# Pooled attention and MLP on one core: more buffers for the MLP, and attention re-packed and issued in a fixed order between its matmuls

## The chip, the core and the metric

The kernel runs on one core of a Trainium2 chip. The metric is the device time of one execution in microseconds (us). A time quoted alone is the median of that kernel's runs. A ratio is the mean time of one kernel's fast runs over the mean of the other kernel's fast runs of the same rounds on the same chip, with a 95% interval, so it is not quite the ratio of the quoted medians. The kernel before was run again in each batch of experiments; its medians there were 440.1 to 445.5 us, and this is why ratios are given beside times.

Names of engines in the profile: PE is TensorE (PEld its weight loads), DVE is VectorE, ACT is ScalarE, POOL is GpSimd, SP only issues DMA in these kernels. To turn a tile means to transpose it.

## The reference

Keys and values are averaged over groups of 8 tokens, so each head has 576 queries against 72 pooled keys. The attention output goes straight into a two-layer MLP with h - tanh(h) between.

```python
B, H, S, D = 8, 8, 576, 64                     # q, k, v, all float32
k_p = k.reshape(B, H, 72, 8, D).mean(axis=3)   # v_p the same
attn = softmax(scale * q @ k_p.T)              # 576 x 72 for each head
x = (attn @ v_p).transpose(0, 2, 1, 3).reshape(4608, 512)
h = x @ w_in                                   # 512 -> 2048
out = (h - tanh(h)) @ w_out                    # 2048 -> 512, float32
```

The MLP is worked in 9 groups of 512 tokens. A group has a **hidden phase** of 16 blocks (four matmuls of 512 columns, a tanh, a subtraction) and an **output phase** of four tiles (16 matmuls of 512 columns each, a copy, a store). This makes 9 x (64 + 64) = 1152 matmuls. A token group can start when the attention output of its tokens lies transposed in `xT`.

## The kernel before

An automatic scheduler orders each engine's instructions. The pools of buffers that matter have one buffer each:

```python
tpool = ctx.enter_context(tc.tile_pool(name="tpool", bufs=1))    # t_sb, tanh
opool = ctx.enter_context(tc.tile_pool(name="opool", bufs=1))    # o_sb
ps_h = ctx.enter_context(tc.tile_pool(name="ps_h", bufs=2, space=bass.MemoryType.PSUM))
ps_o = ctx.enter_context(tc.tile_pool(name="ps_o", bufs=1, space=bass.MemoryType.PSUM))
```

Attention casts q, k and v to bf16 on VectorE, adds four of the eight tokens of a group there, and finishes the pooling with small matmuls against a pooling matrix. It turns q and x on TensorE, and works head by head:

```python
for hp in range(NHP):                     # pairs of heads
    ... matmul k_s1 x PT2, k_bf x PTt     # pooled k, transposed
    ... matmul PT2 x v_s1, PTt x v_bf     # pooled v
    for c in range(NQCH):
        nc.tensor.transpose(qT_ps[...], q_bf[...], ident_bf16[...])
for h in range(H):                        # scores: 72 x 576 for each head
    nc.tensor.matmul(sT_ps[:, s0:s0+n], lhsT=kpT_tiles[hp][pr, :], rhs=qT_tiles[hp][pr, s0:s0+n], ...)
    nc.scalar.activation(out=E_sb[:, :], in_=sT_ps[:, 0:S], func=ACT.Exp, scale=scale)
for qb in range(5):                       # values, 65 columns for each head
    for h in range(H):
        nc.tensor.matmul(x_ps[:rows, h, 0:D+1], lhsT=E_tiles[h][:, s0:s0+rows], rhs=vp_tiles[hp][:, h2, :], ...)
    ... reciprocal, product, four transposes of x, copy into xT
```

```python
for i in range(NHID):                     # hidden phase of a group
    hT_ps = ps_h.tile(...)
    ... four matmuls
    t_sb = tpool.tile([128, TG], FP32, name="t_sb", tag="t_sb")
    nc.scalar.activation(out=t_sb[:, 0:ntok], in_=hT_ps[:, 0:ntok], func=ACT.Tanh)
    gT = gpool.tile([128, TG], BF16, name="gT", tag=f"g{i}")
    nc.vector.tensor_sub(out=gT[:, 0:ntok], in0=hT_ps[:, 0:ntok], in1=t_sb[:, 0:ntok])
```

The softmax here doesn't subtract the row's maximum and nothing guards it: scores larger than these inputs give would overflow.

## Time and profile before

| | before |
|---|---|
| time, median of the first 3 runs | 437.9 us |
| span of the profiled run | 439.6 us |
| first MLP matmul | 65.8 us |
| a hidden block of the last group | every 1.41 us |
| an output tile of the last group | every 4.33 us |

The prediction below shows the lines that this table rests on. In the list of waits a line gives the engine and tile that waited, what ended the wait, the total in us, the number of times and the longest. The list for the kernel before:

```profile
DVE rden L277 <- PE x_ps L269: 21.1, 22, 4.0
DVE vp_aug L225 <- ACT kpT_sb L219: 11.1, 11, 3.0
```

Both are waits of VectorE for attention work of TensorE and ScalarE, and both are small against the 107.9 us that it waited for the tanh.

### The profile page before, as it was taken

The numbers are of one execution on the slowest core, as the hardware profiler recorded it, in microseconds if no ns is written. First come the engines' busy times: TensorE is split into PE (matmuls) and PEld (weight loads), VectorE is DVE, ScalarE is ACT, GpSimd is POOL, SyncE is SP. The second block draws the span as 40 slices with busy tenths as digits, with TensorE's granted clock in tenths as the row PEclk, the third lists the DMA queues.
The fourth block names the chain that finished last, engine by engine and source line by source line (L and its number), as shares of the span: only waits on it lengthen the run. The fifth ranks groups of instructions, "written<-read, shape, count | busy, mean of one in ns | idle before, by whom it ended". The sixth has DMA issues, their size and how long they took to land.

```text
span 439.6 us, 5253 instructions
## 1 busy us (share of the span) xinstructions
PE 361.8 (82%) x2048; PEld 163.7 (37%) x2048; DVE 200.9 (46%) x336; ACT 183.6 (42%) x349; POOL 30.7 (7%) x76
## 2 busy tenths in 40 slices
PE   0006479899799989989999997999999898898875
PEld 0002253444345434544444443444543343333322
DVE  1312656864647544862396339244513523513510
ACT  1003335564366326524562463266535534423321
POOL 7401101100100200020000000000000000000000
PEclk9999999999999989999999998999999999999999
DMA  8999994911930391094002101100011021011012
GB/s 211 227 234 249 317 318 137 264 41 49 275 96 0 74 278 67 2 249 171 0 1 60 38 0 25 48 26 0 26 48 25 0 49 48 0 49 48 1 32 65
DMA packets 34329, 42.29 MB, mean 96 GB/s; under 512 B 1792, under 2 KB 28416, under 8 KB 34304
## 3 DMA queue, kind: packets, MB, share of 16 engines
q1 hardware_dynamic: 30464, 34.61, 28.1%
q0 software_dynamic: 3840, 7.34, 8.5%
q8 instruction: 16, 0.26, 0.3%
q14 instruction: 9, 0.07, 0.1%
HBM read 36.70 MB, written 9.44 MB: 105 GB/s over the span
## 4 chain that ended last, share of the span: by engine, by line
PE 56%; DMA 14%; ACT 13%; DVE 11%; SPq 3%; issue 2%; ACTq 0%; DVEq 0%
PE o_ps L350 22%; PE hT_ps L325 19%; DMA k_raw<-in_k_dram 8%; DVE gT L339 7%; DMA out_dram<-o_sb 7%; ACT t_sb L333 6%; PE sT_ps L245 4%; ACT o_sb L358 3%; SPq L121 3%; PE qps L211 3%; PE x_ps L269 2%; PE xT_ps L286 2%; ACT E_sb L254 1%; PE qps L195 1%; PE qps L202 1%
## 5 line engine op out<-in xcount | busy, mean ns | idle before, releaser
L350 PE MATMUL o_ps<-w2b,gT 128*128 128x512 bf16 x576 | 153.1, 383 | 16.4 <-ACT o_sb L358 11.6
L339 DVE TENSOR_TENSOR gT<-hT_ps,t_sb 128x512 bf16<-128x512 f32 x144 | 99.1, 688 | 143.9 <-ACT t_sb L333 107.9
L325 PE MATMUL hT_ps<-xT,w1b 128*128 128x512 bf16 x576 | 151.1, 385 | 8.4 <-DVE gT L339 8.0
L333 ACT ACTIVATE t_sb<-hT_ps 128x512 f32<-128x512 f32 x144 | 85.6, 595 | 49.1 <-DVE gT L339 42.1
L350 PEld LDWEIGHTS <-gT 128*128 128x128 bf16 x576 | 56.2, 98 | 86.3 <-issue 20.0
L325 PEld LDWEIGHTS <-w1b 128*128 128x128 bf16 x576 | 51.3, 98 | 62.2 <-issue 19.6
L358 ACT COPY o_sb<-o_ps 128x512 f32<-128x512 f32 x36 | 21.1, 586 | 89.4 <-PE o_ps L350 60.7
L254 ACT ACTIVATE E_sb<-sT_ps 72x576 bf16<-72x576 f32 x64 | 41.3, 646 | 33.4 <-PE sT_ps L245 33.3
L245 PE MATMUL sT_ps<-qT_sb,kpT_sb 64*72 64x512 bf16 (+1 forms) x128 | 32.2, 320 | 7.5 <-ACT E_sb L254 7.0
L292 ACT COPY xT<-xT_ps 128x512 bf16<-128x512 bf16 (+1 forms) x40 | 21.8, 544 | 25.9 <-PE xT_ps L286 25.5
L269 PE MATMUL x_ps<-vp_aug,E_sb 72*128 72x65 bf16 (+1 forms) x320 | 28.7, 203 | 0.6 <-ACT E_sb L254 0.6
L279 DVE TENSOR_TENSOR x_sb<-x_ps,rden 128x512 bf16<-128x512 f32 (+1 forms) x40 | 27.4, 685 | 0.8
L219 ACT CAST kpT_sb<-qps 128x72 bf16<-128x72 f32 x32 | 6.9, 217 | 49.1 <-PE qps L211 48.0
L181 PE MATMUL qps<-PT,k_s 128*128 128x64 bf16 x32 | 6.5, 204 | 25.0 <-DVE k_s L162 21.5
L269 PEld LDWEIGHTS <-E_sb 72*128 72x128 bf16 (+1 forms) x320 | 18.8, 104 | 16.6 <-issue 12.1
L245 PEld LDWEIGHTS <-kpT_sb 64*72 64x72 bf16 x128 | 11.1, 114 | 35.0 <-issue 34.5
L211 PE MATMUL qps<-ident_bf,q_bf 128*128 128x128 bf16 (+1 forms) x160 | 22.7, 238 | 0.0
L233 ACT COPY qT_sb<-qps 128x576 bf16<-128x576 bf16 x32 | 20.4, 636 | 4.4 <-DVE vp_aug L225 4.4
L143 DVE CAST k_bf<-k_raw 128x2048 bf16<-128x2048 f32 x8 | 9.8, 1227 | 23.3 <-PE qps L188 11.7
L277 DVE RECIPROCAL rden<-x_ps 128x8 f32<-128x8 f32 (+1 forms) x40 | 8.1, 202 | 21.2 <-PE x_ps L269 21.1
L286 PE MATMUL xT_ps<-ident_bf,x_sb 128*128 128x128 bf16 (+1 forms) x160 | 15.7, 224 | 0.9 <-DVE x_sb L279 0.9
L188 PE MATMUL qps<-PTt,k_bf 64*128 64x8 bf16 x32 | 5.7, 179 | 12.0 <-DVE k_bf L147 12.0
(37 smaller groups left out, 153.3 us busy)
## 6 DMA issues: line engine op xcount, KB each, us to landing
q_raw<-in_q_dram SPq DMA_DIRECT2D x8, 1024.0 KB, 6.2
k_raw<-in_k_dram SPq DMA_DIRECT2D x8, 1024.0 KB, 13.1
v_raw<-in_v_dram SPq DMA_DIRECT2D x8, 1024.0 KB, 13.8
out_dram<-o_sb SPq DMA_DIRECT2D x40, 128.0 KB, 2.4
out_dram<-o_sb SPq DMA_DIRECT2D x16, 256.0 KB, 2.3
w1b<-in_moe_w_in_dram POOLq DMA_DIRECT2D x4, 512.0 KB, 13.7
w2b<-in_moe_w_out_dram POOLq DMA_DIRECT2D x4, 512.0 KB, 20.6
q_raw<-in_q_dram POOLq DMA_DIRECT2D x8, 128.0 KB, 7.7
```

The costliest lines, as they stand in the source:

```text
L211: nc.tensor.transpose(qT_ps[:, c * 128 : c * 128 + rows], q_bf[:rows, c, h0 : h0 + 2, :].rearrange("p h d -> p (h d)"), ident_bf16[:rows, ...
L245: nc.tensor.matmul(sT_ps[:, s0 : s0 + n], lhsT=kpT_tiles[hp][pr, :], rhs=qT_tiles[hp][pr, s0 : s0 + n], start=True, stop=True,)
L254: nc.scalar.activation(out=E_sb[:, :], in_=sT_ps[:, 0:S], func=ACT.Exp, scale=scale,)
L269: nc.tensor.matmul(x_ps[:rows, h, 0 : D + 1], lhsT=E_tiles[h][:, s0 : s0 + rows], rhs=vp_tiles[hp][:, h2, :], start=True, stop=True,)
L279: nc.vector.tensor_mul(out=x_sb[:rows, :, :], in0=x_ps[:rows, :, 0:D], in1=rden[:rows, :, :].to_broadcast([rows, H, D]),)
L286: nc.tensor.transpose(xT_ps[:, fb, 0:rows], x_sb[:rows, 2 * fb : 2 * fb + 2, :].rearrange("p h d -> p (h d)"), ident_bf16[:rows, :rows],)
L292: nc.scalar.copy(out=xT[:, :, pos0 : pos0 + rows], in_=xT_ps[:, :, 0:rows],)
L325: nc.tensor.matmul(hT_ps[:, 0:ntok], lhsT=w1b[:, fb, i * 128 : (i + 1) * 128], rhs=xT[:, fb, tok0 : tok0 + ntok], start=(fb == 0), stop=(f ...
L333: nc.scalar.activation(out=t_sb[:, 0:ntok], in_=hT_ps[:, 0:ntok], func=ACT.Tanh,)
L339: nc.vector.tensor_sub(out=gT[:, 0:ntok], in0=hT_ps[:, 0:ntok], in1=t_sb[:, 0:ntok],)
L350: nc.tensor.matmul(o_ps[:brows, :], lhsT=gts[i][:, tb * 128 : tb * 128 + brows], rhs=w2b[:, i, :], start=(i == 0), stop=(i == NHID - 1),)
L358: nc.scalar.copy(out=o_sb[:brows, :], in_=o_ps[:brows, :])
```

## The change

The intent is to let TensorE run the MLP without bubbles, to give attention fewer and fuller matmuls, and to spread the next batch's attention through the MLP of the present group in an order that is written down. The core of the diff, with cuts:

```diff
-    tpool ... bufs=1    opool ... bufs=1    ps_h ... bufs=2    ps_o ... bufs=1
+    tpool ... bufs=3    opool ... bufs=3    ps_h ... bufs=3    ps_o ... bufs=2    ps_a ... bufs=3
+    ctx.enter_context(tc.manual_schedule())        # program order on every engine
...
+    k_rows = k.rearrange("b h (g j) d -> b (h g) (j d)", j=POOL)   # a row: 8 tokens of one group
+    def pool_kv(b, ke, ve):                        # pooling by adds; GpSimd for b >= 1
+        for eng, r in ((ke, kr), (ve, vr)):
+            eng.tensor_tensor(out=r[:, :, 0:4, :], in0=r[:, :, 0:4, :], in1=r[:, :, 4:8, :], op=ALU.add)
+            eng.tensor_tensor(out=r[:, :, 0:2, :], in0=r[:, :, 0:2, :], in1=r[:, :, 2:4, :], op=ALU.add)
+            ...                                    # last add into kd; for v a product with a 0/1 mask into VB
+    def q_prep(b):
+        nc.vector.tensor_copy(...)                 # cast, two instructions
+        for j in range(R + 1):
+            nc.sync.dma_start_transpose(out=qT[...], in_=q_bf[...])
+    def scores(b, t):                              # 128 (head, group) rows at once, two halves of 288 queries
+        for n, hp in enumerate(PAIRS[t]):
+            nc.tensor.matmul(ps[:, :], lhsT=KB[b % 2][:, hp, t*128:(t+1)*128], rhs=qT[:, hp, ...], ...)
+    def av(b, blk):                                # values, four heads at once
+        ...                                        # reciprocal, product
+        nc.sync.dma_start_transpose(out=xT[...], in_=x_sb[...])
...
+    load_kv(0); load_q(0)
+    pool_kv(0, nc.vector, nc.gpsimd)
+    ...                                            # GpSimd: w1 in four pieces, w2 in four
+    q_prep(0)
+    load_kv(1); load_q(1)                          # SP: behind the transposes of q
+    k_transpose(0); scores(0, 0..4); av(0, 0..4)   # SP: transposes of x behind load 1
+    for g in range(NG):
+        for i in range(NHID):
+            mlp_h(g, i, gts)
+            if i == 1: pool_kv(nb, nc.gpsimd, nc.gpsimd)
+            if i == 3: q_prep(nb); load_kv(nb + 1); load_q(nb + 1)
+            if i == 13: k_transpose(nb)
+        for u in range(16):                        # quarters of the output tiles
+            mlp_o(...)
+            if u < NT: scores(nb, u)
+            if u in (6, 7, 9, 10, 12): av(nb, ...)
```

## The prediction

The forecast's sum came to 341 us, given as 340: start 42, slow first matmuls 2, MLP 248.3, attention on TensorE 31.5, q casts 10, x transposes 3.5, tail 3.6.

- The 31.5 is 7 x 4.5, and the 4.5 was 1.96 for the scores, 2.1 for the values and 0.4 for k. The 2.1 is cut. The trace of the changed kernel shows 0.36 us for the six value matmuls of a block (117.39 to 117.75 us), so 1.8 us for five blocks. The 122 ns of a score matmul stands: in proportion to 0.2155 us for 512 columns it is 0.121 us, and that trace shows four in 0.49 us (112.72 to 113.21 us), 0.1225 us each.
- Of the rivals the reckoning of (a) came to 440 us, and of the first half of (b), 350 us or more. That adds on GpSimd can block a q cast, the second half of (b), was a guess then, since the trace of the kernel before has no add on GpSimd; `a_vadd_dve` below shows it (a cast of 0.41 us took 1.75 beside the adds).

The 2 to 3 us for a transpose by DMA were the author's estimate, from the 2.4 us that a plain 128 KB store takes to land in the kernel before (issue list); the even shares of the engines were an assumption.

> **What bounds the kernel now.** I read the page first: the engines' shares, the chain that ended last, the costliest groups, the slices.
>
> ```profile
> PE 361.8 (82%) x2048; PEld 163.7 (37%) x2048; DVE 200.9 (46%) x336; ACT 183.6 (42%) x349; POOL 30.7 (7%) x76
> PE   0006479899799989989999997999999898898875
> DMA  8999994911930391094002101100011021011012
> PE 56%; DMA 14%; ACT 13%; DVE 11%; SPq 3%; issue 2%; ACTq 0%; DVEq 0%
> L350 PE MATMUL o_ps<-w2b,gT 128*128 128x512 bf16 x576 | 153.1, 383 | 16.4 <-ACT o_sb L358 11.6
> L339 DVE TENSOR_TENSOR gT<-hT_ps,t_sb 128x512 bf16<-128x512 f32 x144 | 99.1, 688 | 143.9 <-ACT t_sb L333 107.9
> L325 PE MATMUL hT_ps<-xT,w1b 128*128 128x512 bf16 x576 | 151.1, 385 | 8.4 <-DVE gT L339 8.0
> L333 ACT ACTIVATE t_sb<-hT_ps 128x512 f32<-128x512 f32 x144 | 85.6, 595 | 49.1 <-DVE gT L339 42.1
> ```
>
> PE looks 82% busy, but a matmul's 383 ns is its latency, not its spacing: the reader has to look at the timeline to see how far PE is from full. The list of waits says who holds whom: tanh and subtraction hold each other.
>
> ```profile
> DVE gT L339 <- ACT t_sb L333: 107.9, 98, 3.3
> ACT t_sb L333 <- DVE gT L339: 42.1, 59, 1.2
> ```
>
> The timeline of the last group (no attention left) shows the loop, and further down the output matmuls.
>
> ```profile
> 408.77 1.02 PE L325 MATMUL hT_ps<-xT,w1b 128*128 128x512 bf16 x4 [0.18 <-DVE gT L339]
> ...
> 408.81 0.60 ACT L333 ACTIVATE t_sb<-hT_ps 128x512 f32<-128x512 f32 x1 [0.82 <-DVE gT L339]
> ...
> 409.44 0.69 DVE L339 TENSOR_TENSOR gT<-hT_ps,t_sb 128x512 bf16<-128x512 f32 x1 [0.72 <-ACT t_sb L333]
> ...
> 410.18 1.02 PE L325 MATMUL hT_ps<-xT,w1b 128*128 128x512 bf16 x4 [0.17 <-DVE gT L339]
> ...
> 427.16 3.61 PE L350 MATMUL o_ps<-w2b,gT 128*128 128x512 bf16 x16 [0.72 <-ACT o_sb L358]
> ...
> 431.49 3.61 PE L350 MATMUL o_ps<-w2b,gT 128*128 128x512 bf16 x16 [0.72 <-ACT o_sb L358]
> ```
>
> Sixteen back-to-back matmuls take 3.61 us, so one takes (3.61 - 0.383) / 15 = 0.215 us. A hidden block (four matmuls) should take 0.862 us of PE, but blocks come every 410.18 - 408.77 = 1.41 us: t_sb has one buffer, so the next tanh waits for the subtraction (0.60 + 0.69 + about 0.12 of handover). An output tile comes every 431.49 - 427.16 = 4.33 us instead of 3.45, as o_ps has one buffer. 144 x 1.41 + 36 x 4.33 = 359 us; the first MLP matmul starts at 65.8 us (timeline); with 4 us of tail that makes 429 of the 439.6. So three things bound it: the one-buffer loops, the start (DMA at 8-9 tenths for six slices), and attention work that partly fills the bubbles.
>
> [...]
>
> **The change part by part.**
>
> *MLP.* t_sb and hT_ps get three buffers, o_ps two. The round trip of one hidden buffer is 1.03 (matmuls) + 0.03 + 0.60 + 0.03 + 0.69 + 0.05 = 2.43 us; over three buffers 0.81 us, just under PE's 0.862. VectorE needs 0.72 per block, ScalarE 0.63. So PE sets the pace: 1152 x 0.2155 = 248.3 us instead of 359.
>
> *Attention on PE.* The instruction order shows 52 matmuls a batch instead of 112, all with full 128x128 weights; the q and x transposes are gone. Scores: 16 x 122 ns = 1.96 us. Values: per row block twice (130, 195, 65 columns), the small ones at 64 ns (eight 65-column matmuls of before take 0.65 us: (0.65 - 0.20) / 7)[...]. k: six at some 64 ns, 0.4 us. Together 4.5 us a batch. In the fixed order this lies wholly on PE's path: 7 x 4.5 = 31.5 us (batch 0 is in the start).
>
> *Attention elsewhere.* ScalarE: ten exps of 288 columns, about 0.42 us each (between 595 ns at 512 and 646 at 576, 0.8 ns per column), spread over five quarter tiles: hidden. VectorE: reciprocal 0.2 + product of 256 columns 0.42 (half of 685 ns, plus fixed cost), ten pairs a batch: 6.2 us in the output phase where it has nothing else: hidden. The q cast is not hidden: 1.21 + 0.40 us between the fourth and fifth subtraction; slack is 0.862 - 0.69 = 0.17 per block, and 0.16 over the three buffers, so PE stands about 1.4 us: 7 x 1.4 = 10 us. The eight small K copies at block 13 come too late in the phase to stop PE.
>
> *GpSimd.* Per batch 1280 + 640 + 640 (k) and 1280 + 640 + 320 + 960 (v) = 5760 elements[...]. It starts when a load lands, in the middle of a hidden phase, and is over before the next q cast: hidden.
>
> *DMA transposes.* q's are due 11 us later: hidden. x's last block that the next group needs (fourth, at quarter 10) has 5 quarters, 4.7 us, for 1.5 us of VectorE and an estimated 2 to 3 us of DMA: about even. I allow 0.5 us a group, 3.5 us.
>
> *Start.* k, v, q of batch 0 (3.54 MB) come first and alone. Before moved two batches and both weights, 7.1 MB + 8.4 MB as read, in some 49 us: 316 GB/s. So q is there at 2 + 11.5 = 13.5 us, cast and turned at 19, scores to 25, values to 32. But the transposes of x stand in the same queue behind the load of batch 1, which shares the engines with the weights (GpSimd issues those only after adding v, at about 17 us). With even shares its 3.54 MB take 7.1 / 0.316 = 22 us, to about 40; turned x at 42. Weights are then complete by 55, before the output phase (42 + 13.8) is deep. MLP starts at 42 instead of 65.8[...]: before's first blocks show 1.46 us for three matmuls; I add 2 us.
>
> *Sum:* 42 + 2 + 248.3 + 31.5 + 10 + 3.5 + tail 3.6 (copy 0.58, store 2.4, handover) = 341; I say 340.
>
> **The rivals.** (a) *Transposes by DMA too slow.* [...] (b) *GpSimd becomes the bound*: [...] Or its additions block the q cast, some 3 us a group: 360. (c) *VectorE as bound in the hidden phase*: 16 x 0.72 + 1.6 + 1.0 = 14.1 us against 13.8: only what I charged; each further 1 us costs 7. (d) *The start is DMA-bound as before*: if batch 1 and weights must all land, 55 us instead of 42: 353. (e) *All hidden*: casts and transposes cost nothing, the loads go faster: 320.
>
> **Range and chances.** Terms that come from the trace (248 + 4 of tail) are firm; start (36 to 55), stalls (0 to 4 us a group, up to 30) and attention (28 to 36) are not. Upwards there are more ways than down: 320 to 366. Same or slower needs rival (a) nearly in full, or two others at once: 3% each.
>
> **What would show it.** Right: a first MLP matmul near 42 us; hidden blocks every 0.86 us; one gap of 1 to 2 us after the fourth block of groups with attention, released by the subtraction; no waits of PE for output copies; PE's groups above 90% to the end, chain over 80% PE. Wrong: PE's first waits in a group released by a DMA of xT (a), by kd or VB from POOL (b), q casts far over 1.2 us (b), or the first hidden matmul or the first output tile waiting for weights past 50 us (d).

## The result and the profile after

The changed kernel took **351.77 us** (median of 4 runs, 350.74 to 353.21), against 440.12 us for the kernel before in the same rounds. The ratio is 0.7998, with a 95% interval from 0.7938 to 0.8058. The profiled run was fast, with a span of 350.2 us and a mean granted TensorE clock of 0.961 (the share of full clock that the chip granted).

First the page of the changed kernel: busy time of each engine, the 40 slices (8.75 us each; a digit is tenths of busy time, for PEclk tenths of full clock), and the chain that ended last.

```profile
PE 287.7 (82%) x1538; PEld 143.3 (41%) x1568; DVE 166.7 (48%) x361; ACT 139.9 (40%) x293; POOL 106.9 (31%) x72
PE   0007002899989998999999899989998999999994
PEclk9999655899999999999999999999999999999999
PE 75%; DMA 9%; SPq 7%; DVE 5%; issue 2%; ACT 1%; ACTq 0%; DVEq 0%
```

PE stands at 8 or 9 from the eighth slice to the last but one. The share of 82% is the same as before, and this shows how little that share says: before, PE's busy time held the latency of matmuls that stood apart (0.38 us each, while back to back they come every 0.2155 us). What is left lies at the left edge. Seven slices go by before PE is busy, the fourth is a short spell of attention, and the chain has 9% of DMA and 7% of SP's queue. The clock digits fall to 5 while PE waits (0.52 from 36 to 59 us).

Next the costliest groups (line, engine, operation, tiles; then busy us, mean ns of one, idle us before them and who ended most of it), and the waits that answer to those of before.

```profile
L256 PE MATMUL hT_ps<-xT,w1b 128*128 128x512 bf16 x563 | 129.8, 384 | 9.5 <-DVE gT L266 6.2
L276 PE MATMUL o_ps<-w2b,gT 128*128 128x512 bf16 x559 | 134.6, 379 | 0.9
L264 ACT ACTIVATE t_sb<-hT_ps 128x512 f32<-128x512 f32 x144 | 85.2, 597 | 72.1 <-PE hT_ps L256 71.9
```

```profile
DVE x_sb L218 <- DMA xT<-x_sb: 22.9, 7, 20.0
PE s_ps L184 <- DMA qT<-q_bf: 16.4, 2, 9.3
```

The tanh now waits for TensorE (71.9 us) and no longer for the subtraction. Output matmuls were idle for 0.9 us in all, instead of 16.4, of which 11.6 were waits for copies. (The counts 563 and 559 should be 576: some matmul records are missing from this trace.) The new waits are for DMA transposes: one of 20 us for x, and two that together make 16.4 us for q. Yet a transpose is quick when little else is under way, as the issue list says (out<-in, engine, count, median us from issue to landing; the line of qT has the same count and median):

```profile
xT<-x_sb SPq DMA_TRANSPOSE x40, 2.4
```

The timeline of a group in the middle (start, duration, engine, line, operation, count, and in brackets the idle time before it):

```profile
131.83 1.22 DVE L102 CAST q_bf<-q_raw 128x2048 bf16<-128x2048 f32 x1
...
134.03 6.20 PE L256 MATMUL hT_ps<-xT,w1b 128*128 128x512 bf16 x27 [0.88 <-DVE gT L266]
```

The group's only stall is the 0.88 us that the q cast costs. The first hidden matmuls of the nine groups come at 58.98, 94.27, 126.94, 159.62, 192.29, 224.96, 257.63, 290.30 and 317.93 us: a period of 32.67 us with attention, 27.63 without.

The timeline of the start, where the time went:

```profile
13.43 1.64 DVE L102 CAST q_bf<-q_raw 128x2048 bf16<-128x2048 f32 x1 [3.24 <-DMA q_raw<-in_q_dram]
...
15.10 6.51 SPq L109 DMA_TRANSPOSE qT<-q_bf  x5
...
19.27 3.20 POOL L322 DMA_DIRECT2D w1b<-in_moe_w_in_dram  x4
...
25.59 10.63 SPq L91 DMA_DIRECT2D q_raw<-in_q_dram  x1
...
27.74 3.76 PE L184 MATMUL s_ps<-qT,KB 128*128 128x288 bf16 x15 [7.18 <-DMA qT<-q_bf]
...
58.98 0.58 PE L256 MATMUL hT_ps<-xT,w1b 128*128 128x512 bf16 x1 [2.48 <-DMA xT<-x_sb]
```

Read it from the top. q is there at 13.43 us, and most of it is cast at 15.1. SP then needs 6.51 us to issue five transposes. The weights are issued at 19.27, and the fourth and fifth transposes land only when the other fifteen score matmuls can go, at 27.7. SP's last issue of the load of batch 1 takes 10.63 us. Behind it in SP's order stand the transposes of x, whose first is issued at 36.31 us, and the first MLP matmul starts at 58.98.

### The profile page after: what moved, and what is told of

It reads as the page before. It is cut to its first block, busy times and chain, and to the rows that moved or that the text cites. A ratio compares the mean times of both kernels' runs of the same rounds, so it can differ in the third digit from the quotient of the medians.

```text
span 350.2 us, 4472 instructions
## 1 busy us (share of the span) xinstructions
PE 287.7 (82%) x1538; PEld 143.3 (41%) x1568; DVE 166.7 (48%) x361; ACT 139.9 (40%) x293; POOL 106.9 (31%) x72
## 4 chain that ended last, share of the span: by engine, by line
PE 75%; DMA 9%; SPq 7%; DVE 5%; issue 2%; ACT 1%; ACTq 0%; DVEq 0%
PE o_ps L276 35%; PE hT_ps L256 31%; DMA xT<-x_sb 6%; PE s_ps L184 4%; PE x_ps L208 4%; SPq L91 3%; DMA q_raw<-in_q_dram 3%; DVE q_bf L102 3%; SPq L109 2%; DVE gT L266 2%; ACT t_sb L264 1%; SPq L79 1%; SPq L83 1%; DVE q_bf L105 1%; PE kT_ps L155 1%
## 5 line engine op out<-in xcount | busy, mean ns | idle before, releaser
L256 PE MATMUL hT_ps<-xT,w1b 128*128 128x512 bf16 x563 | 129.8, 384 | 9.5 <-DVE gT L266 6.2
L276 PE MATMUL o_ps<-w2b,gT 128*128 128x512 bf16 x559 | 134.6, 379 | 0.9
L264 ACT ACTIVATE t_sb<-hT_ps 128x512 f32<-128x512 f32 x144 | 85.2, 597 | 72.1 <-PE hT_ps L256 71.9
L120 POOL TENSOR_TENSOR k_raw<-k_raw 128x1280 f32<-128x1280 f32 x7 | 20.2, 2888 | 138.9 <-DMA k_raw<-in_k_dram 138.9
L285 ACT COPY o_sb<-o_ps 128x512 f32<-128x512 f32 x36 | 21.1, 586 | 92.7 <-PE o_ps L276 80.9
L218 DVE TENSOR_TENSOR x_sb<-x_ps,rden 128x256 bf16<-128x256 f32 x80 | 34.0, 425 | 25.4 <-DMA xT<-x_sb 22.9
L208 PE MATMUL x_ps<-VB,E 128*128 128x130 bf16 (+2 forms) x240 | 22.2, 228 | 21.0 <-DVE x_sb L218 20.7
L184 PE MATMUL s_ps<-qT,KB 128*128 128x288 bf16 x128 | 23.6, 305 | 16.4 <-DMA qT<-q_bf 16.4
L191 ACT ACTIVATE E<-s_ps 128x288 bf16<-128x288 f32 x80 | 28.9, 412 | 17.0 <-PE s_ps L184 16.6
L208 PEld LDWEIGHTS <-E 128*128 128x128 bf16 x240 | 17.5, 101 | 31.2 <-DVE x_sb L218 22.4
L120 POOL TENSOR_TENSOR v_raw<-v_raw 128x1280 f32<-128x1280 f32 x8 | 23.1, 2886 | 8.4 <-DMA v_raw<-in_v_dram 8.3
L137 POOL TENSOR_TENSOR VB<-v_raw,mask 128x960 bf16<-128x960 f32 x8 | 14.4, 1794 | 0.6
## 6 DMA issues: line engine op xcount, KB each, us to landing
w1b<-in_moe_w_in_dram POOLq DMA_DIRECT2D x4, 512.0 KB, 11.6
```

The source lines that it names most:

```text
L120: eng.tensor_tensor(out=r[:, :, 0:4, :], in0=r[:, :, 0:4, :], in1=r[:, :, 4:8, :], op=ALU.add)
L184: nc.tensor.matmul(ps[:, :], lhsT=KB[b % 2][:, hp, t * 128 : (t + 1) * 128], rhs=qT[:, hp, half * hs : (half + 1) * hs], start=(n == 0), s ...
L191: nc.scalar.activation(out=E[:, t, half * hs : (half + 1) * hs], in_=ps[:, :], func=ACT.Exp, scale=SCALE)
L208: nc.tensor.matmul(ps[:, h0 : h0 + s1 - s0, :].rearrange("p h d -> p (h d)"), lhsT=E[:, t, c0 : c0 + 128], rhs=vb[:, t, s0:s1, :].rearrang ...
L218: nc.vector.tensor_tensor(out=x_sb[:, half, :, :], in0=ps[:, :, 0:D], in1=rden[:, :, :].to_broadcast([128, 4, D]), op=ALU.mult,)
L256: nc.tensor.matmul(h_ps[:, :], lhsT=w1b[:, fb, i * 128 : (i + 1) * 128], rhs=xT[:, fb, tok0 : tok0 + TG], start=(fb == 0), stop=(fb == NFB ...
```

## The experiments

Twelve kernels ran; all gave correct results. Each was built from the changed kernel except `b_tsb3`, which was built from the kernel before. The theory at the outset was: *the loops with one buffer held the kernel before (M); in the changed kernel the start is 17 us too late because the transposes stand in one queue with the load of batch 1 (Q)*. The rivals were that the weights must land in any case (W), that buffers of x hold the start, and that attention's new form brought the gain.

| run | what | time, us | ratio to before | first hidden matmul, us |
|---|---|---|---|---|
| changed kernel | | 351.77 | 0.7998 | 58.98 |
| a_bufs_one | one buffer each again | 437.22 | 0.9806 | 58.83 |
| b_tsb3 | before, three t_sb | 456.71 | 1.0237 | 66.30 |
| a_load1_late | load of batch 1 later | 350.88 | 0.7980 | 47.06 |
| a_xsb5 | five x_sb | 350.22 | 0.7969 | 57.64 |
| a_xpe_start | x of batch 0 on TensorE | 339.81 | 0.7730 | 42.22 |
| a_qcast_pool | q casts on GpSimd | 344.58 | 0.7836 | 59.45 |
| a_pe_turns | all turns on TensorE | 344.28 | 0.7729 | 31.30 |
| a_vadd_dve | v of batch 0 on VectorE | 350.95 (one run) | - | 58.93 |
| a_best | several together | 320.32 | 0.7184 | 28.45 |
| a_best2 | and q of batch 1 on TensorE | 324.24 | 0.7339 | 29.42 |
| a_best3 | and load 2 later | 325.15 | 0.7416 | 28.75 |
| a_best4 | or load 2 by GpSimd | 332.41 | 0.7526 | 28.75 |

### Where the gain comes from: one buffer each again

```diff
-    tpool bufs=3, opool bufs=3, ps_h bufs=3, ps_o bufs=2
+    tpool bufs=1, opool bufs=1, ps_h bufs=2, ps_o bufs=1
```

> The changed kernel with the MLP's buffers as before: t_sb 1, o_sb 1, hT_ps 2, o_ps 1. Theory M (the buffers carry most of the gain): the hidden loop falls back to 1.41 us a block, 144 x 0.55 = 79 us more, output tiles lose up to 0.6 us each, about 20, and the q cast hides in the slack, 6 less: 440 to 450 us. Rival O (the fixed order of the attention carries it): below 400 us.

It took 437.22 us (436.54 to 437.44), ratio 0.9806 (0.9753 to 0.9859). Of the 0.200 that the changed kernel gains on before, 0.181 is gone again. Waits and timeline of this run:

```profile
ACT t_sb L264 <- DVE gT L266: 107.5, 126, 1.5
```

```profile
106.29 1.02 PE L256 MATMUL hT_ps<-xT,w1b 128*128 128x512 bf16 x4 [0.39 <-DVE gT L266]
107.70 1.02 PE L256 MATMUL hT_ps<-xT,w1b 128*128 128x512 bf16 x4 [0.39 <-DVE gT L266]
```

The block comes every 1.41 us, exactly as in the kernel before, and the tanh waits for the subtraction again. In this order of instructions the buffers carry nearly all of the gain; which of the four buffer counts does most was not separated. All the rest of the change, without them, is worth 2%, and that is a balance of a gain and a loss. The last group, without attention, takes 38.3 us here (392.81 to 431.06) and 34.4 in the kernel before (400.68 to 435.10), because the scheduler of the kernel before puts matmuls of the first output tile into the gaps of the hidden loop, and the fixed order doesn't. From the last group of the kernel before:

```profile
409.63 0.38 PE L350 MATMUL o_ps<-w2b,gT 128*128 128x512 bf16 x1
```

### The reverse: three tanh buffers in the kernel before

```diff
-    tpool = ctx.enter_context(tc.tile_pool(name="tpool", bufs=1))
+    tpool = ctx.enter_context(tc.tile_pool(name="tpool", bufs=3))
```

> The kernel before with three t_sb buffers instead of one and nothing else[...]. Theory M: tanh no longer waits for the subtraction, the hidden loop is then held by two hT_ps buffers, 2.43 / 2 = 1.21 us instead of 1.41 a block: up to 29 us off where no attention fills the gap, 412 to 425 us. Rival O: within 2% of 440.

This was a miss: 456.71 us (455.6 to 457.11), 2.4% *slower* than before (ratio 1.0237, 1.0169 to 1.0306). The loop itself did what was expected. Near the end of the timeline of this run four blocks take 4.86 us (from 393.90 to 398.76), 1.21 us each; the first of them and the one after the fourth:

```profile
393.90 1.02 PE L325 MATMUL hT_ps<-xT,w1b 128*128 128x512 bf16 x4
...
398.76 1.02 PE L325 MATMUL hT_ps<-xT,w1b 128*128 128x512 bf16 x4
```

But the automatic scheduler gave another order. In the two traces, sorted by start, 1333 of TensorE's 2048 matmuls come from another line than the matmul at the same place before. The waits of VectorE for attention grew:

```profile
DVE vp_aug L225 <- ACT kpT_sb L219: 75.8, 22, 10.4
DVE rden L277 <- PE x_ps L269: 48.7, 15, 16.0
```

Before these were 11.1 and 21.1 us. So in the changed kernel the buffers are needed for the gain, but three t_sb alone don't bring it to the kernel before. What is missing there (the other three buffer counts, the fixed order or the re-packed attention) no run separates. That the new order causes the loss is an inference from the two lists of waits; I did not run before's order with three buffers. A second cost was left out: the granted clock of this run was 0.959 on average, against 0.992 in the kernel before (0.94 to 0.96 in the four stretches from 66 to 400 us, against 0.98 to 1.00). Between 200 and 210 us, where TensorE was busy for 6.18 us of 10, it was 0.66, and eight hidden matmuls took 3.57 us instead of 1.89. How the loss divides between waits and clock stays open.

### The start: load of batch 1 later

```diff
     q_prep(0)
-    load_kv(1); load_q(1)
     k_transpose(0); scores(0, 0..4); av(0, 0..4)
+    load_kv(1); load_q(1)
```

> The changed kernel with the load of batch 1 issued behind the x transposes of batch 0. Theory Q (the x transposes waited because they stood behind that load in the same queue): the first x transpose lands by 42 to 45 us instead of 55, the first hidden matmul comes at about 45 instead of 59. The load then ends with the weights at about 56, so the q cast in group 0 waits for it, and the hidden phase of group 0 ends near 67 instead of 77: about 342 us. Rival W (the engines are full of weights and any small transfer waits for them, wherever it stands): first hidden matmul at 52 or later, 348 us or more.

The first hidden matmul came at 47.06 us, 12 us earlier and close to theory Q, but the time was 350.88 us (349.6 to 351.58), the same as without the change. The timeline of this run shows where the 12 us went:

```profile
60.05 3.87 POOL L120 TENSOR_TENSOR v_raw<-v_raw 128x1280 f32<-128x1280 f32 x1
61.09 3.10 DVE L105 CAST q_bf<-q_raw 64x512 bf16<-64x512 f32 x1
...
64.85 5.41 PE L256 MATMUL hT_ps<-xT,w1b 128*128 128x512 bf16 x14 [9.00 <-DVE gT L266]
```

q of batch 1 now lands late. Its cast stands in VectorE's fixed order after the fourth subtraction of group 0, and TensorE stands for 9.00 us behind it. The tail of the cast took 3.10 us beside a GpSimd add, where it takes 0.41 us in later groups, and that add 3.87 us instead of 2.88. The hidden phase of group 0 ended at about 75 us, against 77 in the changed kernel: 12 us were gained and 10 lost within one phase. Of the 10, 9.00 are the stall, in place of 0.88, and 2 more come from matmuls that ran slowly after it: the 27 hidden matmuls from 64.85 us on (the line shows the first 14) took 8.43 us, at a granted clock of 0.56 up to 70 us, against 6.20 in later groups. Theory W isn't quite out either: the x transposes, with no load ahead of them, still took 7.9 us to land (median) beside the weights, against 2.4 later. The start 12 us earlier gained nothing beyond the spread of the runs (350.88 against 351.77), as an instruction in the middle of the fixed order waited for a late load.

### The start: more buffers for x

```diff
-        x_sb = work.tile(..., tag="x_sb", bufs=3)
+        x_sb = work.tile(..., tag="x_sb", bufs=5)       # and q_bf: one buffer, to make room
```

> The changed kernel with five x_sb buffers instead of three (q_bf goes to one buffer to make room). The list of waits names the product into x_sb as the longest wait at the start (20 us). Rival B (the buffers hold the start): the five blocks are done at 36 us and the first hidden matmul comes well before 50, 340 us or less. Theory Q (the transposes themselves land late): the wait moves from VectorE to the hidden matmul, which waits for xT until about 57 us; gain 1 to 2 us, 350 us.

It took 350.22 us. All five blocks of x were done at 38.0 us, and the wait only moved:

```profile
57.64 0.58 PE L256 MATMUL hT_ps<-xT,w1b 128*128 128x512 bf16 x1 [20.92 <-DMA xT<-x_sb]
```

The list of waits of the changed kernel names x_sb (20.0 us), but a fourth and fifth buffer are of no use when the matmul that follows needs the same transposes.

### The start: x of batch 0 turned on TensorE

```diff
+        if b == 0:
+            ... four nc.tensor.transpose into PSUM, one nc.scalar.copy into xT
+            return
         nc.sync.dma_start_transpose(out=xT[...], in_=x_sb[...])
```

> The changed kernel with the x blocks of batch 0 alone turned on TensorE and copied by ScalarE, so that no DMA lies between the attention of batch 0 and the MLP. Theory Q: first hidden matmul at about 39 us; then the q cast of batch 1, in order on VectorE, waits for its load (lands at about 52) and holds the hidden phase, which ends near 62 instead of 77: 337 us. If the bytes alone bound the start (rival D: batch 1 and weights have to land before anything runs on), the time stays above 345.

It took 339.81 us (339.1 to 340.17), 12 us less than the changed kernel, near the expected 337. The first hidden matmul came at 42.22 us, 3 us later than expected, as the five blocks (product, transposes, copy) run one after another at 2.0 us each. The tail of q's cast still waited for its load, 2.99 us on TensorE:

```profile
53.87 7.89 PE L268 MATMUL hT_ps<-xT,w1b 128*128 128x512 bf16 x27 [2.99 <-DVE gT L278]
```

Here load 1 keeps its place, and the gain stays. Together with `a_load1_late` this shows the cause of the late start: the transposes of x, small in themselves, stood in SP's queue behind 3.5 MB of loads that shared the engines with the weights (43.2% of their time for SP's queue and 74.0% for that of the weights, from 21.7 to 55.5 us in the changed kernel). A smaller part is the weights alone, as the 7.9 us there show.

### The stall in each group: q casts on GpSimd

```diff
-        nc.vector.tensor_copy(out=q_bf[...], in_=t[...])      # two of them
+        ce = nc.vector if b == 0 else nc.gpsimd
+        ce.tensor_copy(out=q_bf[...], in_=t[...])
```

> The changed kernel with the q cast of batches 1 to 7 on GpSimd instead of VectorE. Theory C: the 0.88 us that PE stands after block 4 of each group with attention goes away, 7 x 0.88 = 6 us: 346 us. Rival: GpSimd's casts[...] come late or block VectorE, and the time stays at 351 or rises.

It took 344.58 us (343.98 to 344.97), against the 346 expected. The 0.88 us gap is gone, with the hidden phase up to the k matmuls in one piece:

```profile
125.21 12.25 PE L257 MATMUL hT_ps<-xT,w1b 128*128 128x512 bf16 x54
```

The period fell from 32.67 to 31.63 us (125.21 to 156.84), so a q cast on VectorE costs 1.04 us a group. GpSimd's own casts take 1.89 and 0.61 us and are hidden.

### All turns on TensorE

```diff
-        nc.sync.dma_start_transpose(...)          # q and x, all batches
+        ... four nc.tensor.transpose, one ScalarE copy for each block
```

> The changed kernel with q and x of all batches turned on TensorE and copied by ScalarE (no DMA transposes). Forty 128-column transposes a batch at about 0.08 us (five take 0.53 us in the trace of before) come onto PE's path: 7 x 3.2 = 22 us more, some stalls by copies 5; at the start x(0) no longer waits in the queue, 15 less: 358 to 366 us. Rival: the copies hold ScalarE and cost more than that, above 375; or PE hides them, below 350.

Expected to be slower, it was faster: 344.28 us (343.73 to 345.87), ratio 0.7729. The steady cost was somewhat below the expected 22 + 5 us: the period is 35.06 us (71.31 to 106.37), 2.4 us more than with DMA transposes, 17 us in seven groups. But the first hidden matmul came at 31.30 us, 28 us earlier, where 15 were expected. Group 0 then took 40 us, 5 more than a later one: TensorE stood for 1.8 us for w1, 1.0 for a subtraction and 2.3 for w2:

```profile
PE o_ps L313 <- DMA w2b<-in_moe_w_out_dram: 2.3, 3, 1.0
```

Group 1 starts 23 us earlier than in the changed kernel (71.31 against 94.27). So DMA transposes lose 23 us up to the end of group 0 and earn 14 in the six groups after it, which makes the 9 us between the two spans (350.2 and 341.6); each belongs where it pays.

### Did GpSimd's adds slow the first q cast?

```diff
-    pool_kv(0, nc.vector, nc.gpsimd)                       # k on VectorE, v on GpSimd
+    pool_kv(0, nc.vector, nc.vector, lambda: q_prep(0))    # v on VectorE behind the q cast
```

> The changed kernel with the adds of v of batch 0 moved from GpSimd to VectorE, behind the q cast; GpSimd keeps the last multiplication, so the weights are still issued near 19 to 20 us. In the changed kernel the two q casts of batch 0 took 1.64 and 1.75 us beside GpSimd adds, in later batches 1.22 and 0.41. Theory lock (GpSimd adds hold the casts up): 1.22 and 0.41 us here (within 0.05), no matter that loads are still landing. Rival (the loads landing at that time, or a first execution, slow them): 1.6 and 1.7 us as before. Either way the five transposes are issued one after another at 1.26 us each and the start gains little: first hidden matmul between 56 and 60 us, time 348 to 353 us.

One look (350.95 us, of unknown state), for the durations only:

```profile
13.88 1.23 DVE L102 CAST q_bf<-q_raw 128x2048 bf16<-128x2048 f32 x1 [3.39 <-DMA q_raw<-in_q_dram]
15.02 0.41 DVE L105 CAST q_bf<-q_raw 64x512 bf16<-64x512 f32 x1
```

Without a GpSimd add beside them the casts took 1.23 and 0.41 us, instead of 1.64 and 1.75, in this one run: the adds did hold the casts up. But that is not a cause of the late start, as the issue of the transposes began at 15.1 us and took 6.51 us in both kernels, and the first hidden matmul came at 58.93 us.

### A version that uses what was learned, and three attempts to better it

`a_best` turns q and x of batch 0 on TensorE, casts q of batch 0 on ScalarE, issues load 1 directly behind load 0 and w1 between two GpSimd adds, keeps DMA transposes for the later batches, and casts their q on GpSimd.

> Improved version: batch 0's q and x turned on TensorE, its q cast on ScalarE, load of batch 1 directly behind that of batch 0, w1 issued after the first v addition, q casts of batches 1 to 7 on GpSimd, batch 1's q step late in group 0. First hidden matmul at about 30 us, hidden phase of group 0 over at about 47 (77 in the changed kernel), no stall after block 4: about 315 us. If the bytes bind (15.5 MB as read[...]): output phase of group 0 waits for w2, about 320.

It took **320.32 us** (318.85 to 321.55), ratio 0.7184, the fastest kernel here. The first hidden matmul came at 28.45 us and the period was 31.63 us. Group 0 still took 39.7 us (28.45 to 68.16). From its timeline:

```profile
49.48 0.40 PE L228 MATMUL s_ps<-qT,KB 128*128 128x288 bf16 x1 [5.92 <-DMA qT<-q_bf]
```

The transposes of q of batch 1 stand beside w2 and land late: their issues run from 40.26 to 47.37 us, and the nine up to 75 us took a median of 4.2 us to land, against 2.4 over the whole run. So the 320 us named for the case that bytes bind came out, but with a wait for q and not for w2. `a_best2` takes them out of the queue:

```diff
-                q_prep(nb)                                        # cast, DMA transposes
+                if nb > 1: q_prep(nb)
+                if nb == 1 and i in (10, 12, 14): q_turn(1, ...)  # TensorE; two more after block 15
```

> The 320 us version with q of batch 1 also turned on TensorE (20 small matmuls, cast on GpSimd between the adds of batch 1), so that nothing that the scores of batch 1 need stands behind the weights in the queues. If the transposes behind the weights were the cause of the 5.9 us wait: no wait of the first scores for qT, group 0 about 35 us instead of 39.7, time 315 to 317. If w2 itself were late, PE waits for w2b at the first output tile instead and the time stays at 319 to 321.

It missed: 324.24 us (322.24 to 325.41), slower than `a_best`. The wait for qT is gone, but without the transposes SP had nothing left to hold back the load of batch 2. It was issued from 19.2 us on instead of 47.5 (the 23.2 us in the text below is the second of its six issues), and now w2 was late:

```profile
PE o_ps L323 <- DMA w2b<-in_moe_w_out_dram: 5.3, 3, 2.8
```

`a_best3` then issues the load of batch 2 behind the first output tile's store:

> The version with q of batch 1 on TensorE, and the load of batch 2 issued behind the store of the first output tile. In that version the SP queue, freed of the transposes, issued the load of batch 2 from 23.2 us on, beside the weights, and PE then waited 5.3 us for w2 (324 us). If the bytes of batch 2 ahead of w2 were the cause: no wait for w2b over 1 us, group 0 in 34 to 36 us, time 314 to 318. If w2 is late for another reason (its own queue): PE still waits about 5 us for w2b and the time stays at 320 to 324.

As expected the waits for w2 were gone, but not as expected the time was 325.15 us (324.49 to 327.31; the record calls the verdict on this ratio unclear, as four of the seven runs of the kernel before were slow in its batch). Now the load stood ahead of the x transposes of batch 1, as in the changed kernel's start:

```profile
PE x_ps L252 <- DVE x_sb L262: 8.5, 3, 7.9
```

`a_best4` lets GpSimd issue that load behind w2:

> As the version with q of batch 1 on TensorE, but the load of batch 2 is issued by GpSimd directly behind w2, so that it stands neither beside w2 (324 us, 5.3 us of waits for w2b) nor ahead of the x transposes in the SP queue (325 us, 8.5 us of waits for x_sb). If order among the transfers is all that cost those two versions: group 0 in 34 to 36 us with no wait of PE over 1.5 us in it, time 314 to 318. Rival: issuing six loads keeps GpSimd busy for 5 us or[...] until w2 has landed; then kd or VB of batch 1 is late, PE waits for it over 3 us, and the time is 318 to 326.

The rival came true: 332.41 us. (Its 5 us is an estimate: an issue of w1 took 0.8 us in the changed kernel, 3.20 us for four.) GpSimd issued five of the six loads only after waits of 1.37 to 4.71 us, each until a piece of the weights had landed. Its adds and the q cast behind them came late, and TensorE, in its fixed order, stood for 16 us. From the timeline of this run:

```profile
35.05 0.79 POOL L79 DMA_DIRECT2D v_raw<-in_v_dram  x1 [4.71 <-DMA w1b<-in_moe_w_in_dram]
...
54.41 0.61 PE L133 MATMUL qT_ps<-ident,q_bf 128*128 128x128 bf16 x4 [15.99 <-POOL q_bf L120]
```

So the 5.92 us were never bettered. Each of the three versions took away one wait and got another: all moved the same bytes of load 2 and the weights, only in another order. That load 2 could be placed better still was not shown.

## Why the prediction was right or wrong

The predicted 340 us (320 to 366) against 351.8 us: right in direction and range, with the main mechanism right and one term badly mis-sized. That the total came nearer than its worst term is luck: 17 us too little for the start and 10 too much for attention and stalls have opposite signs. Term by term, from the starts of the groups in the changed kernel's profiled run:

| term | predicted, us | measured, us |
|---|---|---|
| start, to the first MLP matmul | 42 | 59.0 |
| slow first matmuls | 2 | 2.6 (group 0 took 35.29, later ones 32.67) |
| MLP | 248.3 | 248.7 (nine times 27.63) |
| attention and stalls in seven groups | 31.5 + 10 + 3.5 = 45 | 35.3 (seven times 32.67 - 27.63) |
| tail | 3.6 | 4.6 |
| sum | 341 | 350.2 |

**The MLP was right.** Three buffers were just enough for TensorE to set the pace, and the spacing of 0.2155 us held (27.63 us for 128 matmuls, 0.216 each). With one buffer each the time came back to 437 us. The prediction's sum for the kernel before was misread, though: 16 x 1.41 + 4 x 4.33 = 39.9 us a group counts the first output tile twice, since its matmuls stand in the gaps of the hidden loop (the line at 409.63 us above). The last two groups took 34.1 and 34.4 us (from 366.60, 400.68 to 435.10), so the MLP is an estimated 9 x 34.3 = 309 us and not 359, and about 60 of the 439.6 us were attention in the gaps after the start. The forecast did not use the 359.

**The start was the step that failed**, by 17 us: its signs were a first MLP matmul near 42 us and a chain over 80% PE, and it came at 59 with 75%. "q is there at 13.5 us" held (13.43). "Turned at 19" did not: the last scores could start at 27.7. The prediction gave the transposes 2 to 3 us each to land, which is right alone (2.4 us, median of 40), but left out that each takes about 1.3 us of SP to issue (6.51 us for five; a load of k, v or most of q takes a median of 0.5 to 0.6, though q's last piece takes 2.1), and that the last two fell beside the weights. An issue can also wait: SP's last one for load 1 took 10.63 us, and the trace of the kernel before already held load issues of 9.93 and 13.77 us on SP. "With even shares" failed too. From 21.7 to 55.5 us the DMA view gives the queue of the weights 74.0% of the engines' time and SP's queue 43.2%, so the weights had 63% and not half (the two sum to 117%, so the packets' times overlap). The load ran until about 50 us instead of 40. The transposes of x, rightly seen "in the same queue behind the load of batch 1", were given 2 us after it; their issues ran from 36.31 to 58.98, the longest took 8.2 us, and the last two blocks waited for a free x_sb buffer until the first transpose had landed. In its result this is rival (d), 55 us for the start. But the cause is not that everything must land, since `a_xpe_start` and `a_best` begin the MLP at 42 and 28 us with the same bytes to move. The cause is the place of small transposes behind large loads. The traces show it: the slowest x transpose took 19.1 us with load 1 ahead of it and 10.5 us with the load moved behind the transposes (medians of the five 10.5 and 7.9), where the median of all 40 is 2.4.

**The slow first matmuls were about right.** In the kernel before, where the 1.46 us for three was read, the granted clock stood at 1.00 (65 to 70 us), so that trace does not show a low clock as the cause. In the changed kernel the first three hidden blocks came every 1.71 us, 427 ns a matmul, twice the later 0.2155 us; this lasted about 5 us, from 59 to 64, at a granted clock of 0.50. The clock record doesn't explain every such spell: in `a_xpe_start` the first 15 hidden matmuls took 6.07 us while it stood at 1.00.

**Attention and stalls were over-estimated by 10 us.** The q cast was estimated at 1.4 us a group and measured 0.88 as a gap and 1.04 as a period difference. Attention on TensorE takes 31.63 - 27.63 = 4.0 us (period of `a_qcast_pool`) instead of 4.5. The x transposes cost nothing in the steady state, where 0.5 was allowed.

**The rivals.** (a) was wrong in the steady state, and what it feared happened at the start, for another reason: the queue. (b) was wrong: GpSimd needs 13.0 us a batch, in a period of 32.67. An add of 1280 elements takes 2.89 us (2.26 ns an element). Its additions did block a q cast, by 2.7 us in `a_load1_late`, but in the changed kernel only in the start, where it did not matter. (c) was right in kind: the cast is all that VectorE costs. (e) was not reached; `a_best` gets its time, with another start.

## What to carry to other kernels

Count a DMA transpose not by how long it takes alone but by what stands ahead of it in its queue (here a median of 2.4 us over all 40, and of 10.5 for the five behind load 1); in the start, where loads fill the queues, turn small tiles on TensorE, and use the DMA where the queues are idle. In a fixed order, check for every instruction that waits on a load what stands behind it: an earlier start gained 12 us here and lost nearly all of them to one cast that waited. And look at the order of instructions when you add buffers: three tanh buffers for one are part of what gains 18% in the changed kernel, while alone in the kernel before, with the order that the scheduler then chose, they cost 2%.
